# Attention, mish FFN and top-1 experts on one core: narrower expert slots, all weight splits on VectorE, logits in another buffer, the last slot's tiles one by one

## The chip, the cores and the metric

The kernel runs on one core of one Trainium2 chip. The metric is device time in microseconds of one execution, the median of several. Engines are named as in the profile: PE (TensorE, with its weight loads as PEld), DVE (VectorE), ACT (ScalarE), POOL (GpSimd) and SP (SyncE, which issues most DMAs).

## The reference

```python
def reference(q, k, v, w_in, w_out, w_gate, w_output_gate, w1, w2):
    # attention: 4 batches, 8 heads, 576 tokens, head size 64
    # heads 0-3: causal, window 32; heads 4-7: causal, every 4th key, window 128
    x = softmax(mask(q @ k.T / 8)) @ v            # -> x: 2304 x 512
    h = x @ w_in                                  # 512 -> 2048
    x = (h * tanh(log1p(exp(h)))) @ w_out         # 2048 -> 512
    logits = x @ w_gate                           # 8 experts
    e = argmax(logits); p = softmax(logits)[e]
    s = sigmoid(x @ w_output_gate)[e]
    return p * s * (relu(x @ w1[e]) @ w2[e])      # 512 -> 1024 -> 512
```

All data is float32.

## The kernel before, in words

**Precision.** Every float32 operand of a large matmul is split in two float32r parts, hi (a copy that ACT rounds) and lo (the difference), and a product takes three matmuls, hi·hi, hi·lo and lo·hi (PASS). `split` (L331) does it for a piece: ACT L332 writes hi, and L334 subtracts on DVE, or on POOL where `pool_lo` is set.

**First part (up to about 578 us).** The 2304 tokens go through in eight half-batches of 288. A step g is one block of 128 hidden columns of one half-batch: `l1` (L388, 12 matmuls of 288 columns into one of two PSUM tiles `hps`), the mish chain (ACT L395 exp, DVE L396, DVE L400, ACT L406 and L407, DVE L412, which frees `hps`, then `split` into ghi and glo), and, LAG = 3 steps later, `l2` (L431, 12 matmuls). The attention of the next half-batch is cut in small operations, and a hand-written loop (`take`) puts some of them between the halves of `l1` and `l2`. PE, DVE and ACT each run their instructions in the order in which the program was scheduled, so a late operation holds all behind it on its engine.

**Routing.** After a half-batch's last step its logits are made in pieces: `logits1` (8 matmuls of the transposed form, ACT L484 evicts them into the tile `lgT`), `logits2` (three transposes back, L491), `route1` and `route2` (the choice and each token's row number), `route3` (L555 transposes of 96 tokens, DVE L561 or ACT L559 copies them into a tile `row`, DVE L562 and L563 append the scale and the token's number) and `route4` (L582: POOL scatters the 96 rows into the DRAM array `buf`, which has a region of 2304 rows for each expert). The tiles `row`, `lgT`, `fill`, some gathered rows `xs` and the output rows `eo` all share one ring of three buffers (pool `rp`, tag "row"). `setup_rows` (L126) fills the first MOST rows of each region with zeros and an invalid token number.

**Experts (from about 578 us).** A slot is one expert, taken in order of its number of tokens; the expert of rank 2 comes first (slot 0: 256 rows at once, 128 late ones in `e_l1_late` with hi and lo side by side). CAPS gives each slot's number of rows; tokens above a cap go through the loop in `rest` (L808), which runs zero times on this input. Expert weights come in 64 loads of 512 KB (`e_load`, SP L664 and L667, a ring of four buffers shared with other loads), each split in two halves of 128x512 (`e_split`). Of the 128 halves 36 are subtracted on POOL: pieces 1, 3, 5 and 7 of slot 0 and pieces 3 and 7 of the other slots. The first eight pieces are split in the last steps of the first part. `e_l1` (L730) is 12 matmuls for each of 8 blocks f, with CAPS[q] moving columns; ACT L734 and DVE L735 evict. In slots 1, 3, 4 and 5 (COLUMNS) `e_l2` holds weights and moves CAPS[q] columns (L764, 12 matmuls a block, then transposes L803); in the others it holds the tokens and moves 512 weight columns (L772). `e_row` scales a tile of rows (ACT L780) and POOL scatters it to the output (L781).

Of the kernel before, what the change touches and what calls it, by code (L numbers as in the profile page):

```python
# [9 lines left out]
F32 = mybir.dt.float32  # L10
# [18 lines left out]
def tile_attn_mish_moe(ctx, tc, qkv, w_in, w_out, w_gate, w_og, w1, w2, out):  # L29
# [12 lines left out]
    NCH = HS // CH  # L42
    NP = HS // DIL
    ROW = DM + 2
    FCAP = 384
    CAPS = [FCAP, 440, 384, 336, 312, 288, 256, 256]
    PRE = 256
    COLUMNS = (1, 3, 4, 5)
    EGB = 2
# [278 lines left out]
                                       op0=ALU.logical_shift_right, op1=ALU.bitwise_or)  # L328
        return f.bitcast(F32)

    def split(hi, lo, src, pool_lo=False):  # L331
        nc.scalar.activation(out=hi, in_=src, func=AF.Copy)  # L332
        eng = nc.gpsimd if pool_lo else nc.vector
        eng.tensor_tensor(out=lo, in0=src, in1=hi.bitcast(F32), op=ALU.subtract)  # L334

    def w_split(n):
        kind, f = pieces[n]
# [136 lines left out]
    def logits1(j):  # L474

        R = rt[j]
        hl = R.pop("hl")
        ps = ps_a.tile([4 * E, HS], F32, tag="a", name="lgT")
        for kk in range(KD):
            for x in range(2):  # L480
                nc.tensor.matmul(out=ps, lhsT=wgs[:, kk, :], rhs=hl[x][:, kk, :],
                                 start=(kk == 0 and x == 0), stop=(kk == KD - 1 and x == 1))
        R["lgT"] = rp.tile([128, ROW], F32, tag="row", name="lgT")[0:4 * E, 0:HS]
        nc.scalar.activation(out=R["lgT"], in_=ps, func=AF.Copy)  # L484

    def logits2(j):
# [180 lines left out]
            nc.sync.dma_start(out=t.rearrange("p (k f) -> p k f", k=2), in_=src.rearrange("o (k p) f -> p (o k) f", p=128))  # L667
        es[q, i] = t

    def e_split(q, i, pool_lo=False):  # L670
        kind, hf = divmod(i, 4)
        if hf == 0:
            for a in range(2):
                ew[q, kind, a] = wp.tile([128, 4096], F32R, tag="w", name="we")
        c = slice(1024 * hf, 1024 * hf + 1024)
        t, hi, lo = es.pop((q, i)), ew[q, kind, 0][:, c], ew[q, kind, 1][:, c]
        if pool_lo:
            for h in (slice(0, 512), slice(512, 1024)):
                split(hi[:, h], lo[:, h], t[:, h], True)
        else:  # L680
            for c in (0, 512):
                split(hi[:, c:c + 512], lo[:, c:c + 512], t[:, c:c + 512], False)

    es_seq = [(q, i) for q in range(E) for i in range(NPC)]
    nload = [0]
# [7 lines left out]
    def e_splits_to(n, last=E * 8):  # L693
        while nsplit[0] < min(n, last, len(es_seq)):
            i = nsplit[0]
            e_loads_to(min(i + 3, last))
            e_split(*es_seq[i], pool_lo=i % 8 in ((1, 3, 5, 7) if i < 8 else (3, 7)))
            nsplit[0] += 1
            e_loads_to(min(i + 4, last))

# [36 lines left out]

    def e_l1_late(f, x):

        ps = ps_h.tile([128, 2, 128], F32, tag="h", name="eh")  # L740
        for kk in range(KD):
            c = kk * F2 + 128 * f
            for a in range(2):
                nc.tensor.matmul(out=ps, lhsT=ew[0, 0, a][:, c:c + 128], rhs=x[:, kk],
                                 start=(kk == 0 and a == 0), stop=(kk == KD - 1 and a == 1))
        t = mg.tile([128, 128], F32, tag="lt", name="lt", bufs=2)
        nc.vector.tensor_copy(t, ps[:, 0])
        nc.vector.tensor_tensor(out=t, in0=ps[:, 1], in1=t, op=ALU.add)
        g = mg.tile([128, 2, 128], F32R, tag=("egh", "egl")[f % 2], name="eg")
        gh, gl = g[:, 0], g[:, 1]  # L750
        nc.scalar.activation(out=gh, in_=t, func=AF.Relu)
        nc.vector.scalar_tensor_tensor(out=gl, in0=t, scalar=0.0, in1=gh.bitcast(F32), op0=ALU.max, op1=ALU.subtract)
        gt["e", 0, f] = (gh, gl)

    def e_l2(q, f, part):

# [16 lines left out]
                                 rhs=ew[q, 1, a][:, DM * f:DM * f + DM],  # L773
                                 start=(f == 0 and n == 0), stop=(f == NF2 - 1 and n == 2))

    def e_row(q, i, m, src):

        x = meta[q, 0][0:m, i // 128, :]
        o = rp.tile([128, DM], F32, tag="row", name="eo")
        nc.scalar.activation(out=o[0:m], in_=src, func=AF.Copy, scale=x[:, 0:1])  # L780
        ins = nc.gpsimd.indirect_dma_start(  # L781
            out=out[:, :], out_offset=bass.IndirectOffsetOnAxis(ap=x.bitcast(I32)[:, 1:2], axis=0),
            in_=o[0:m], in_offset=None, bounds_check=NT - 1, oob_is_err=False)
        apart("out", ins)
# [20 lines left out]
        return [lambda i=i, m=m: turn(i, m) for i, m in part]  # L805


    def rest():  # L808

        cnt = chosen["cnt"]  # L810
        caps = sm.tile([128, E], F32, name="caps")
# [27 lines left out]
        nc.vector.tensor_copy(rv, ri)  # L839
        mo_ctx.close()  # L840
        ot = ctx.enter_context(tc.tile_pool(name="ot", bufs=1, reuse_waits="tile"))
        n = nc.values_load(tn[0:1, 0:1], min_val=0, max_val=NT // 128 + E)
        w1r = w1.rearrange("e d f -> (e d) f")
        w2r = w2.rearrange("e f d -> (e f) d")
        with tc.For_i(0, n, 1):
# [60 lines left out]
    if True:  # L906
# [37 lines left out]
        for g in range(total + LAG):  # L944
            if g in begin:
                j, due = begin[g]
                pend += attention(j)
                rate[0] = len(pend) / (4 * NF)
                credit[0] = 0
            if g < total:  # L950
                j, f = steps[g][:2]
            nq = -(-len(pend) // max(1, due - g)) if g < total else 0

            def take(at):
                if 2 * NF <= g < total - NF:
                    credit[0] += rate[0]
                    n = int(credit[0] + 1e-6)
                    credit[0] -= n
                else:
                    n = (nq + 4 - at) // 4  # L960
                for _ in range(n):
                    if pend:
                        pend.pop(0)()
                for op in at_slot.pop((g, at), []):
                    op()
            w_to(max((i + 1 for i, x in enumerate(need) if x <= g), default=0), 80)
            if g < total:
                l1(g, 0)
                take(4)
                l1(g, 1)  # L970
            if 0 < g <= total:
                mish_c(g - 1)
            if g < total:
                mish_a(g)
            take(1)
            if 0 < g <= total:
                mish_d(g - 1)
            if g >= LAG:
                l2(g - LAG, 0)
                take(3)  # L980
                l2(g - LAG, 1)
                jj, ff, _, lst, _ = steps[g - LAG]
                if lst:
                    route0(jj)
                    if ff == NF - 1 and jj < NH - 1:
                        logits0(jj)
                        rq = routing(jj)
                        if jj == NH - 2:
                            rq += [choose_first, first_load, lambda: first_tr(0), lambda: first_tr(1)]
                        when, slot = (ROUTE, 4) if jj < NH - 2 else (ROUTE_SOON, 2)  # L990
                        for i, op in enumerate(rq):
                            at_slot.setdefault((g + 1 + when[i], slot), []).append(op)
            if g < total:
                mish_b(g)
            take(2)
            if g == FILLS - 6:
                nc.sync.dma_start(out=wg[:, :, 0:E], in_=w_gate.rearrange("(k p) e -> p k e", p=128))
                nc.sync.dma_start(out=wg[:, :, E:2 * E], in_=w_og.rearrange("(k p) e -> p k e", p=128))
            if g == FILLS:
                split(wgs[:, :, 0:2 * E], wgs[:, :, 2 * E:], wg, False)  # L1000
            if FILLS <= g < FILLS + E:
                setup_rows(g - FILLS)
            if j == NH - 1 and f >= 6 and g < total:
                e_splits_to(f - 7, 8)
# [8 lines left out]
        for f in range(NF2 + 1):  # L1013
            if f < NF2:
                e_l1(0, f, PRE, first[0], first[1], gp, (("ghi", 2), ("glo", 2)))
            if f >= 1:
                e_l2(0, f - 1, pre)
            if f == 4:
                (li, lm), = late
                x_load(0, li, lm, rp, "row")  # L1020
                xl = stp.tile([128, KD, 2, 128], F32R, tag="st", name="xl")
            if f == 7:
                x_tr(0, li, lm, xl[:, :, 0, :], xl[:, :, 1, :])
            e_splits_to(8 + f - 4)
# [6 lines left out]
    if True:  # L1031
# [23 lines left out]
        for q in range(1, E):  # L1055
# [5 lines left out]
            for f in range(NF2 + 1):  # L1061
                if f < NF2:
                    e_l1(q, f, CAPS[q], exh[q], exl[q], mg, (("egh", EGB), ("egl", EGB)))
                    e_splits_to(8 * (q + 1) + f + 1)
                if f >= 1:
                    e_l2(q, f - 1, tiles(q))
                if outs and f >= 1:
                    outs.pop(0)()
                if ops and f >= 3:
                    ops.pop(0)()  # L1070
            while ops:
                ops.pop(0)()
            outs = e_out(q, tiles(q))
    rest()


_INS = ['qkv', 'moe_w_in', 'moe_w_out', 'moe2_w_gate', 'moe2_w_output_gate', 'moe2_w1', 'moe2_w2']
# [59 lines left out]
```

## Time and profile before

| | |
|---|---|
| median of 3 runs | 842.54 us (842.39 to 846.82) |
| the profiled execution | 846.02 us |
| its span | 844.3 us |
| PE busy | 805.8 us, 95% of the span |
| DVE busy | 558.3 us, 66% |
| ACT busy | 501.8 us, 59% |
| POOL busy | 105.5 us, 12% |

The profile is of one execution, the second row of this table; 1.72 us of its time lie outside the span, and the median is 3.48 us under it. Shares of busy time are means over very different stages, so the prediction reads windows of the span and what each engine waited for there.

### The profile page before, as it was taken

The numbers are of one execution on the slowest core, as the hardware profiler recorded it, in microseconds if no ns is written. First come the engines' busy times: TensorE is split into PE (matmuls) and PEld (weight loads), VectorE is DVE, ScalarE is ACT, GpSimd is POOL, SyncE is SP. The second block draws the span as 40 slices with busy tenths as digits, with TensorE's granted clock in tenths as the row PEclk, the third lists the DMA queues.
The fourth block names the chain that finished last, engine by engine and source line by source line (L and its number), as shares of the span: only waits on it lengthen the run. The fifth ranks groups of instructions, "written<-read, shape, count | busy, mean of one in ns | idle before, by whom it ended". The sixth has DMA issues, their size and how long they took to land.

```text
span 844.3 us, 16623 instructions
## 1 busy us (share of the span) xinstructions
PE 805.8 (95%) x6205; PEld 751.9 (89%) x6205; DVE 558.3 (66%) x1473; ACT 501.8 (59%) x1419; POOL 105.5 (12%) x109
## 2 busy tenths in 40 slices
PE   7899999798999999999999999989999999999994
PEld 5779998798999999999999999989889989999993
DVE  5979999777767757767767767784772535543610
ACT  3677877675667667667666666661662644644611
POOL 4000000001100100100100000231240313313400
PEclk8989999899999999999999999999999999999997
DMA  9722459411110110111111000521882626536300
GB/s 344 271 80 75 151 159 312 121 37 60 53 55 31 53 56 30 51 39 49 44 35 58 23 10 2 181 73 48 285 286 68 212 82 234 171 113 228 123 24 18
DMA packets 39837, 91.69 MB, mean 109 GB/s; under 512 B 4643, under 2 KB 12835, under 8 KB 39756
## 3 DMA queue, kind: packets, MB, share of 16 engines
q1 hardware_dynamic: 36508, 81.16, 29.6%
q0 software_dynamic: 3248, 9.46, 3.3%
q8 instruction: 49, 0.80, 0.4%
q14 instruction: 32, 0.26, 0.1%
HBM read 73.91 MB, written 17.41 MB: 108 GB/s over the span
## 4 chain that ended last, share of the span: by engine, by line
PE 68%; DVE 12%; DMA 6%; issue 5%; ACT 5%; POOL 1%; SPq 1%; POOLq 0%; ACTq 0%; DVEq 0%
PE hps L388 20%; PE acc L431 19%; PE eh L730 8%; PE ecol L764 6%; DMA wst<-in_moe_w_in_dram 3%; PE o L264 3%; DMA est<-in_moe_w_dram 3%; PE eacc L772 2%; PE sc L218 2%; ACT pr L229 2%; PE tp L246 2%; DVE we L334 2%; ACT we L332 1%; DVE pr L226 1%; DVE nm L227 1%
## 5 line engine op out<-in xcount | busy, mean ns | idle before, releaser
L388 PE MATMUL hps<-xhi,w 128*128 128x288 f32 x1024 | 239.7, 306 | 6.4 <-DVE e L412 6.2
L388 PEld LDWEIGHTS hps<-xhi,w 128*128 128x128 f32 x1024 | 175.2, 191 | 11.7 <-DVE e L412 7.0
L431 PE MATMUL acc<-ghi,w 128*128 128x288 f32 x1024 | 172.5, 302 | 2.3 <-DVE x2T L449 1.3
L388 PE MATMUL hps<-xlo,w 128*128 128x288 f32 x512 | 153.0, 299 | 0.4 <-DVE xlo L271 0.3
L431 PEld LDWEIGHTS acc<-ghi,w 128*128 128x128 f32 x1024 | 145.9, 190 | 8.1 <-DVE x2T L449 2.3
L730 PE MATMUL eh<-exh,we 128*128 128x256 f32 (+5 forms) x448 | 108.6, 316 | 0.0
L388 PEld LDWEIGHTS hps<-xlo,w 128*128 128x128 f32 x512 | 98.2, 192 | 2.2 <-DVE xlo L271 1.8
L431 PE MATMUL acc<-glo,w 128*128 128x288 f32 x512 | 92.8, 297 | 3.1 <-DVE glo L334 3.1
L332 ACT ACTIVATE we<-est 128x512 fp32r<-128x512 f32 x128 | 74.4, 624 | 33.3 <-PE eh L730 16.4
L406 ACT ACTIVATE e<-e,two 128x288 f32<-128x288 f32 x128 | 68.1, 532 | 36.9 <-DVE e L400 36.0
L395 ACT ACTIVATE e<-hps 128x288 f32<-128x288 f32 x128 | 51.6, 404 | 55.0 <-PE hps L388 55.0
L334 DVE TENSOR_TENSOR we<-est,we 128x512 fp32r<-128x512 f32 x92 | 66.1, 755 | 25.2 <-ACT we L332 25.2
L431 PEld LDWEIGHTS acc<-glo,w 128*128 128x128 f32 x512 | 76.6, 190 | 3.7 <-DVE glo L334 3.4
L730 PEld LDWEIGHTS eh<-exh,we 128*128 128x128 f32 x448 | 77.2, 188 | 1.3
L332 ACT ACTIVATE ghi<-e 128x288 fp32r<-128x288 f32 x128 | 56.0, 438 | 31.9 <-PE acc L431 21.7
L582 POOL DMA_INDIRECT buf<-row,si x24 | 22.5, 936 | 417.5 <-DVE si L547 245.4
L735 DVE SCALAR_TENSOR_TENSOR eg<-eh,eg 128x256 fp32r<-128x256 f32 (+5 forms) x64 | 31.0, 484 | 64.2 <-ACT eg L734 64.1
L334 DVE TENSOR_TENSOR glo<-e,ghi 128x288 fp32r<-128x288 f32 x128 | 59.1, 462 | 20.1 <-PE acc L431 10.5
L412 DVE SCALAR_TENSOR_TENSOR e<-e,hps 128x288 f32<-128x288 f32 x128 | 57.4, 448 | 22.1 <-ACT e L407 21.8
L229 ACT ACTIVATE pr<-pr,nm 96x128 f32<-96x128 f32 (+2 forms) x168 | 62.0, 370 | 13.3 <-DVE nm L227 12.9
L730 PE MATMUL eh<-exl,we 128*128 128x256 f32 (+5 forms) x224 | 69.7, 311 | 0.0
L764 PE MATMUL ecol<-eg,we 128*128 128x440 f32 (+3 forms) x384 | 65.4, 320 | 0.5 <-DVE eg L735 0.5
(196 smaller groups left out, 1313.9 us busy)
## 6 DMA issues: line engine op xcount, KB each, us to landing
est<-in_moe_w_dram SPq DMA_DIRECT2D x64, 512.0 KB, 4.2
wst<-in_moe_w_in_dram SPq DMA_DIRECT2D x16, 512.0 KB, 9.6
wst<-in_moe_w_out_dram SPq DMA_DIRECT2D x16, 512.0 KB, 4.4
qkv<-in_qkv_dram SPq DMA_DIRECT2D x12, 608.0 KB, 3.6
qkv<-in_qkv_dram SPq DMA_DIRECT2D x14, 496.0 KB, 3.3
buf<-fill SPq DMA_DIRECT2D x8, 771.0 KB, 8.1
xs<-buf SPq DMA_DIRECT2D x19, 257.0 KB, 4.0
scq<-in_qkv_dram SPq DMA_DIRECT2D x4, 608.0 KB, 10.2
```

Source lines behind the costliest of these rows:

```text
L229: nc.scalar.activation(out=pr[:, h, u, :], in_=src[:, u, :], func=AF.Exp, bias=nm[0:m, h, u:u + 1], accum_out=su[0:m, h, u:u + 1])
L264: nc.tensor.matmul(out=o[64 * h:64 * h + 64, u, :], lhsT=vv, rhs=st["t", h][:, u, :], start=True, stop=True, skip_group_check=True)
L332: nc.scalar.activation(out=hi, in_=src, func=AF.Copy)
L334: eng.tensor_tensor(out=lo, in0=src, in1=hi.bitcast(F32), op=ALU.subtract)
L388: nc.tensor.matmul(out=hps[g], lhsT=w[:, a, kk, 128 * fl:128 * fl + 128], rhs=(xhi, xlo)[x][j][:, kk, :], start=(kk == 0 and n == 0), stop ...
L395: nc.scalar.activation(out=e, in_=hps[g], func=AF.Exp)
L406: nc.scalar.activation(out=r, in_=r, func=AF.Ln, scale=0.2, bias=two5)
L412: nc.vector.scalar_tensor_tensor(out=u, in0=u, scalar=2.5, in1=hps.pop(g), op0=ALU.subtract, op1=ALU.mult)
L431: nc.tensor.matmul(out=accs[j][m], lhsT=w[:, a, fl, 128 * m:128 * m + 128], rhs=gg[x], start=(first and n == 0), stop=(last and n == 2))
L730: nc.tensor.matmul(out=ps, lhsT=ew[q, 0, a][:, c:c + 128], rhs=(hi, lo)[x][:, kk, 0:n], start=(k == 0), stop=(k == 3 * KD - 1))
L735: nc.vector.scalar_tensor_tensor(out=gl, in0=ps, scalar=0.0, in1=gh.bitcast(F32), op0=ALU.max, op1=ALU.subtract)
L764: nc.tensor.matmul(out=accs["e", q][k], lhsT=ew[q, 1, a][:, c:c + 128], rhs=gg[x], start=(f == 0 and n == 0), stop=(f == NF2 - 1 and n == 2))
```

## The change

- `CAPS` goes from [384, 440, 384, 336, 312, 288, 256, 256] to [384, 424, 368, 336, 304, 280, 256, 232], and MOST, its largest, from 440 to 424.
- `split` loses `pool_lo`: all 128 halves of the expert weights are subtracted on DVE.
- `lgT` moves from the ring "row" of three buffers to the ring "pt" of two, which the attention's transposed probabilities use.
- In the last slot (q = 7) the `e_l2` matmuls of blocks 6 and 7 are done for one tile of rows after the other (`e_l2_end`), each tile's rows written right after; the second tile's eviction is shared by DVE and ACT.
- `rest` is cut in two: the count of tokens above the caps is made after slot 6, the loop stays at the end. `e_l1_late` takes its width from FCAP - PRE, which is 128 as before.

```diff
-    CAPS = [FCAP, 440, 384, 336, 312, 288, 256, 256]
+    CAPS = [FCAP, 424, 368, 336, 304, 280, 256, 232]
...
-    def split(hi, lo, src, pool_lo=False):
+    def split(hi, lo, src):
         nc.scalar.activation(out=hi, in_=src, func=AF.Copy)
-        eng = nc.gpsimd if pool_lo else nc.vector
-        eng.tensor_tensor(out=lo, in0=src, in1=hi.bitcast(F32), op=ALU.subtract)
+        nc.vector.tensor_tensor(out=lo, in0=src, in1=hi.bitcast(F32), op=ALU.subtract)
...
-        R["lgT"] = rp.tile([128, ROW], F32, tag="row", name="lgT")[0:4 * E, 0:HS]
+        R["lgT"] = ap.tile([4 * E, HS], F32, tag="pt", name="lgT")
         nc.scalar.activation(out=R["lgT"], in_=ps, func=AF.Copy)
...
-            e_split(*es_seq[i], pool_lo=i % 8 in ((1, 3, 5, 7) if i < 8 else (3, 7)))
+            e_split(*es_seq[i])
...
+    def e_l2_end(q, part):
+
+        for t, (i, m) in enumerate(part):
+            for f in (NF2 - 2, NF2 - 1):
+                for n, (a, x) in enumerate(PASS):
+                    nc.tensor.matmul(out=accs["e", q][t], lhsT=gt["e", q, f][x][:, i:i + m],
+                                     rhs=ew[q, 1, a][:, DM * f:DM * f + DM], start=False, stop=(f == NF2 - 1 and n == 2))
+            e_row(q, i, m, accs["e", q][t], t)
...
-    def e_row(q, i, m, src):
+    def e_row(q, i, m, src, alt=0):
...
-        nc.scalar.activation(out=o[0:m], in_=src, func=AF.Copy, scale=x[:, 0:1])
+        if alt % 2:
+
+            nc.vector.tensor_scalar(out=o[0:m, 0:DM // 2], in0=src[:, 0:DM // 2], scalar1=x[:, 0:1], scalar2=None, op0=ALU.mult)
+            nc.scalar.activation(out=o[0:m, DM // 2:], in_=src[:, DM // 2:], func=AF.Copy, scale=x[:, 0:1])
+        else:
+            nc.scalar.activation(out=o[0:m], in_=src, func=AF.Copy, scale=x[:, 0:1])
...
-                if f >= 1:
+                if f >= 1 and (q < E - 1 or f < NF2 - 1):
                     e_l2(q, f - 1, tiles(q))
...
-            outs = e_out(q, tiles(q))
-    rest()
+            if q < E - 1:
+                outs = e_out(q, tiles(q))
+                if q == E - 2:
+                    left = rest_count()
+            else:
+                e_l2_end(q, tiles(q))
+    rest(*left)
```

The first place is DVE's queue in the last steps of the first part, where slot 0's weights `we` are split among the mish chain (`e`) and its splits (`glo`). Before:

```order
L412 SCALAR_TENSOR_TENSOR e<-e,hps 128x288
L396 TENSOR_SCALAR e<-e 128x288
L400 TENSOR_TENSOR e<-e 128x288
L334 TENSOR_TENSOR we<-est,we 128x512
L334 TENSOR_TENSOR glo<-e,ghi 128x288
L334 TENSOR_TENSOR we<-est,we 128x512
L412 SCALAR_TENSOR_TENSOR e<-e,hps 128x288
L396 TENSOR_SCALAR e<-e 128x288
```

And in the change:

```order
L412 SCALAR_TENSOR_TENSOR e<-e,hps 128x288
L334 TENSOR_TENSOR we<-est,we 128x512
L396 TENSOR_SCALAR e<-e 128x288
L334 TENSOR_TENSOR we<-est,we 128x512
L400 TENSOR_TENSOR e<-e 128x288
L334 TENSOR_TENSOR glo<-e,ghi 128x288
L334 TENSOR_TENSOR we<-est,we 128x512 x3
L412 SCALAR_TENSOR_TENSOR e<-e,hps 128x288
```

The halves that POOL did now stand in DVE's own queue: five instead of two between two L412 here, and one of them between L412 and the next step's L396.

The second place is the ACT queue where `lgT` of the second half-batch is evicted, with the semaphores that each instruction waits for (DMASW0 is the queue of a POOL scatter). Before:

```order
L406 ACTIVATE e<-e,two_109 128x288 [waits DVE_49]
L407 ACTIVATE e<-e 128x288 [waits Activation_49]
L484 ACTIVATE lgT<-lgT 32x288 [waits DMASW0_49,PE_49]
L395 ACTIVATE e<-hps 128x288 [waits PE_49]
L406 ACTIVATE e<-e,two_109 128x288 [waits DVE_49]
```

And in the change:

```order
L406 ACTIVATE e<-e,two_109 128x288 [waits DVE_49]
L407 ACTIVATE e<-e 128x288 [waits Activation_49]
L484 ACTIVATE lgT<-lgT 32x288 [waits PE_49]
L395 ACTIVATE e<-hps 128x288 [waits PE_49]
L406 ACTIVATE e<-e,two_109 128x288 [waits DVE_49]
```

ACT no longer waits for the scatter. DVE's queue at the same place, in the change (before, the copy of the ids waited for DMASW1, the scatter after that one):

```order
L561 COPY row<-rows 96x512 [waits PE_49]
L412 SCALAR_TENSOR_TENSOR e<-e,hps 128x288 [waits Activation_49]
L563 COPY row<-ids 96x1 [waits DMASW0_49]
L396 TENSOR_SCALAR e<-e 128x288 [waits Activation_49]
L400 TENSOR_TENSOR e<-e 128x288 [waits DVE_49]
```

So the copy of the ids still waits for a scatter, the one that ACT waited for before.

## Rows read from the trace of the kernel before

**Rows 1.** Part 1 of the page: busy time of each engine over the span.
```profile
PE 805.8 (95%) x6205; PEld 751.9 (89%) x6205; DVE 558.3 (66%) x1473; ACT 501.8 (59%) x1419; POOL 105.5 (12%) x109
```

**Rows 2.** Windows: length, PE, PEld, DVE, ACT, POOL busy (count), granted clock, DMA share, GB/s.
```profile
145.00:160.00 15.00, 10.61 (x73) 9.59 (x72) 10.35 (x25) 8.29 (x20) 0.00 (x0) 0.77 0.71 214
204.50:215.36 10.86, 8.93 (x64) 8.10 (x63) 5.66 (x22) 5.38 (x24) 0.91 (x1) 0.84 0.26 100
211.00:213.00 2.00, 2.00 (x10) 1.66 (x10) 1.93 (x6) 1.01 (x5) 0.00 (x0) 0.50 0.00 0
273.43:280.32 6.89, 6.89 (x63) 6.45 (x62) 5.39 (x23) 5.71 (x26) 0.00 (x0) 1.00 0.01 2
547.00:563.00 16.00, 12.58 (x89) 11.65 (x88) 15.46 (x23) 11.43 (x26) 8.24 (x7) 1.00 0.34 98
595.00:605.00 10.00, 8.76 (x51) 7.11 (x51) 7.06 (x13) 7.15 (x15) 5.10 (x4) 1.00 0.67 215
605.00:832.00 227.00, 226.32 (x1427) 212.80 (x1427) 105.77 (x211) 105.25 (x213) 54.51 (x45) 1.00 0.46 154
```

**Rows 3.** Chain of waits: start, length, engine, output, line, count; slots 1 and 5.
```profile
623.32 2.40 PE ecol L764 x12
...
762.57 1.60 PE eh L730 x12
```

**Rows 4.** Timeline of PE in slot 7: start, length, instruction; 12 matmuls from the first to the second.
```profile
819.86 0.28 PE L730 MATMUL eh<-exh,we 128*128 128x256 f32 x1
...
821.28 1.54 PE L772 MATMUL eacc<-we,eg 128*128 128x512 f32 x6
```

**Rows 5.** Timeline of PE, last steps of the first part: in brackets idle before, and releaser.
```profile
549.31 0.40 PE L388 MATMUL hps<-xhi,w 128*128 128x288 f32 x1 [0.63 <-DVE e L412]
...
553.92 0.40 PE L388 MATMUL hps<-xhi,w 128*128 128x288 f32 x1 [1.18 <-DVE e L412]
...
558.86 0.40 PE L388 MATMUL hps<-xhi,w 128*128 128x288 f32 x1 [1.48 <-DVE e L412]
```

**Rows 6.** DVE by line and form, 545 to 562 us: busy, mean ns, idle before.
```profile
L400 DVE TENSOR_TENSOR e<-e 128x288 f32<-128x288 f32 x4 | 5.8, 1444 | 0.1
...
L396 DVE TENSOR_SCALAR e<-e 128x288 f32<-128x288 f32 x4 | 3.2, 810 | 0.7 <-ACT e L395 0.6
```

**Rows 7.** The same view, 563 to 575 us, where POOL splits nothing.
```profile
L400 DVE TENSOR_TENSOR e<-e 128x288 f32<-128x288 f32 x3 | 1.4, 459 | 0.1
L396 DVE TENSOR_SCALAR e<-e 128x288 f32<-128x288 f32 x2 | 0.6, 310 | 0.9 <-ACT e L395 0.9
```

**Rows 8.** One half's price: DVE timeline in slot 1, then POOL by line and form.
```profile
625.75 3.69 DVE L334 TENSOR_TENSOR we<-est,we 128x512 fp32r<-128x512 f32 x6
...
L334 POOL TENSOR_TENSOR we<-est,we 128x512 fp32r<-128x512 f32 x36 | 49.2, 1387 | 133.8 <-ACT we L332 133.7
```

**Rows 9.** Waits of SP's DMA queue from 570 us: total, times, longest.
```profile
SPq L667 <- POOL we L334: 17.4, 7, 4.7
```

**Rows 10.** Timeline where `lgT` of the second half-batch is evicted.
```profile
208.06 0.40 ACT L484 ACTIVATE lgT<-lgT 32x288 f32<-32x288 f32 x1 [4.18 <-DMA buf<-row,si]
...
208.52 0.93 PE L218 MATMUL sc<-qkv 64*72 64x104 f32 x14 [1.93 <-ACT lgT L484]
208.66 0.15 DVE L563 COPY row<-ids 96x1 int32<-96x1 int32 x1 [3.96 <-DMA buf<-row,si]
...
219.83 0.46 DVE L412 SCALAR_TENSOR_TENSOR e<-e,hps 128x288 f32<-128x288 f32 x1
```

**Rows 11.** Timeline of the end.
```profile
829.71 2.97 PE L772 MATMUL eacc<-we,eg 128*128 128x512 f32 x12
...
832.02 1.39 ACT L780 ACTIVATE eo<-eacc,meta 128x512 f32<-128x512 f32 x2 [1.72 <-PE eacc L772]
...
834.26 0.98 POOL L781 DMA_INDIRECT out_dram<-eo,meta  x1 [0.31 <-issue]
```

**Rows 12.** PE by line and form: attention scores, plain float32, 48 matmuls in the program.
```profile
L218 PE MATMUL sc<-qkv 64*72 64x104 f32 x96 | 6.0, 257 | 1.9 <-ACT lgT L484 1.9
```

More of the change, by code (lines that the diff above doesn't have):

```diff
@@ L668, in e_load, with e_split @@
         es[q, i] = t
-    def e_split(q, i, pool_lo=False):
+    def e_split(q, i):
         kind, hf = divmod(i, 4)
@@ L676, in e_split @@
         t, hi, lo = es.pop((q, i)), ew[q, kind, 0][:, c], ew[q, kind, 1][:, c]
[L677 to L682, printed above, removed]
+        for c in (0, 512):
+            split(hi[:, c:c + 512], lo[:, c:c + 512], t[:, c:c + 512])
     es_seq = [(q, i) for q in range(E) for i in range(NPC)]
@@ L738, in e_l1_late @@
     def e_l1_late(f, x):
-        ps = ps_h.tile([128, 2, 128], F32, tag="h", name="eh")
+        m = FCAP - PRE
+        ps = ps_h.tile([128, 2, m], F32, tag="h", name="eh")
         for kk in range(KD):
@@ L745, in e_l1_late @@
                                  start=(kk == 0 and a == 0), stop=(kk == KD - 1 and a == 1))
-        t = mg.tile([128, 128], F32, tag="lt", name="lt", bufs=2)
+        t = mg.tile([128, m], F32, tag="lt", name="lt", bufs=2)
         nc.vector.tensor_copy(t, ps[:, 0])
         nc.vector.tensor_tensor(out=t, in0=ps[:, 1], in1=t, op=ALU.add)
-        g = mg.tile([128, 2, 128], F32R, tag=("egh", "egl")[f % 2], name="eg")
+        g = mg.tile([128, 2, m], F32R, tag=("egh", "egl")[f % 2], name="eg")
         gh, gl = g[:, 0], g[:, 1]
@@ L805, in e_out, with rest_count @@
         return [lambda i=i, m=m: turn(i, m) for i, m in part]
-    def rest():
+    def rest_count():
         cnt = chosen["cnt"]
@@ L829, in rest @@
         nc.vector.tensor_copy(tn, tf)
+        return cnt, rem, nc.values_load(tn[0:1, 0:1], min_val=0, max_val=NT // 128 + E)
+    def rest(cnt, rem, n):
         li = sm.tile([128, 13], I32, name="li")
@@ L841, in rest @@
         ot = ctx.enter_context(tc.tile_pool(name="ot", bufs=1, reuse_waits="tile"))
-        n = nc.values_load(tn[0:1, 0:1], min_val=0, max_val=NT // 128 + E)
         w1r = w1.rearrange("e d f -> (e d) f")
@@ L999, in tile_attn_mish_moe @@
             if g == FILLS:
-                split(wgs[:, :, 0:2 * E], wgs[:, :, 2 * E:], wg, False)
+                split(wgs[:, :, 0:2 * E], wgs[:, :, 2 * E:], wg)
             if FILLS <= g < FILLS + E:
@@ L1020, in tile_attn_mish_moe @@
                 x_load(0, li, lm, rp, "row")
-                xl = stp.tile([128, KD, 2, 128], F32R, tag="st", name="xl")
+                xl = stp.tile([128, KD, 2, FCAP - PRE], F32R, tag="st", name="xl")
             if f == 7:
```

## The prediction

> **What bounds the kernel now.** I read the busy shares first: PE is busy 95% of the span and no other engine over 66% [rows 1]. So time is either PE's own work or one of its few waits, and the next view was the windows, to find where PE has holes [rows 2]. In the expert stage, 605 to 832 us, it is busy 226.32 of 227: what counts there is the number of columns that PE moves. Holes lie in three places that the change touches: 145 to 160 (transfers, granted clock 0.77), 204.5 to 215.36 (routing of the second half-batch) and 547 to 563 (the last steps of the first part). For the holes I read the timeline of PE and of the engine that it waited for [rows 5, 10], for prices the chain [rows 3] and groups by form [rows 6 to 8]. The sum is made against the profiled execution, 846.02 us; the median is 3.48 less.
>
> **Narrower slots.** Twelve matmuls of 440 columns take 2.40 us, twelve of 288 take 1.60 [rows 3]: 0.200 and 0.133 each, so 0.44 ns a column and no fixed part to speak of. Slot 1 loses 16 columns in 192 matmuls (both layers move tokens), slot 2 loses 16 in the 96 of its first layer, slots 4 and 5 lose 8 in 192 each: 7680 columns, 3.36 us. The second layers of slots 2 and 7 move 512 weight columns and gain nothing. Slot 7 loses 24 columns in 96 matmuls, from 256 to 232. At 256 columns twelve took 821.28 - 819.86 = 1.42 us, 0.118 each [rows 4]; by the slope the 96 save 1.0. No row shows a large float32r matmul under 256 columns, so this gain is bounded by 0 (the pace stays) and 1.0; I take 0.8, since the slope held over the whole range that rows show. Together **4.2 us**, and PE leaves nearly no idle time that could swallow it [rows 2]. The tokens all still fit, so the loop at the end stays empty; moving its count is free, as the engines do it beside PE's matmuls.
>
> The Trainium skill, page "TensorE: Matmul & The Clock Gate", section "Back-to-back issue gap", has the spacing of matmuls set by the weight load and the matmul together; it would put slot 7's gain anywhere under 1.0, which the bounds above hold already, and no run here shows the size.
>
> **Splits off POOL, last steps of the first part.** Between 547 and 563 DVE is busy 15.46 of 16 us [rows 2], and PE waited for DVE's L412, which frees its PSUM tile, 0.63, 1.18 and 1.48 us: 3.29 in all [rows 5]. DVE is full there because its own operations are slow while POOL splits: L400 takes 1.444 us on average against 0.459 a little later, L396 0.810 against 0.310 [rows 6, 7]. Four of each make 3.94 and 2.00: 5.9 us of DVE lost to eight halves on POOL of 1.387 each [rows 8]. The change puts these eight on DVE at 0.615 us (six in 3.69 [rows 8]): 4.9 us added for 5.9 removed. So DVE's work falls by about one microsecond, and I expect a step of it to be about 3.3 us where PE needs 3.2 plus what else it is given. The order shows five halves between two L412 in the first of these steps, 3.1 us of work, so a part of the wait may stay there. Between 0 and 3.3 I take **2.9 us**, nearest to the rows' balance of work.
>
> The Trainium skill, page "SBUF — State Buffer", section "Who interferes with whom", says that a DVE instruction with two SBUF inputs contends with a GpSimd instruction that reads SBUF, and that the loser of the shared port pair waits for all of it. The trace agrees in kind (L400 three times as long); as full blocking the eight halves would cost DVE 8 x 1.387 = 11.1 us, more than the 5.9 that these rows show, and the term would rise only to its end of 3.3, since PE waited no more than that.
>
> **Splits off POOL, later.** From 595 to 605 PE is busy 8.76 of 10 [rows 2] and waits for slot 0's last weights, some split on POOL at more than twice DVE's price: I take **0.4**, ends -0.5 (DVE's queue is late instead) and 1.2 (the whole hole). From 605 on DVE takes the other halves, 28 of the 36: at 0.615 about 17 us on top of 105.77 busy in 227, which fits on average. SP's queue waited 17.4 us for POOL before it could issue weight loads [rows 9]; that goes, but PE's missing time is 0.7 in all, so earlier weights are worth nothing. **0**, ends +0.7 and -3 (below).
>
> **The logits' buffer.** ACT's L484 waited 4.18 us for a scatter that still held a buffer of the ring, DVE's L563 3.96 for the next one; PE stood 1.93 [rows 10], and just after, the granted clock was 0.50, the 1.2 GHz level, from 211 to 213 [rows 2]. From 204.50 to 215.36 it did 64 matmul records in 10.86 us; the same stretch of a later half-batch took 6.89 for 63 [rows 2]: 3.97 us lost, the upper end. The change frees ACT, but DVE's queue still has the copy of the ids behind a scatter, now the first of the two, which landed at 208.06 where the second landed at 208.66 [rows 10]. So DVE is let go some 0.6 us earlier, and the mish chain behind it (L396, L412, then `hps`) with it; ACT is 4 us earlier with the attention's work. The lower end is 0.6. Whether PE still pauses long enough to lose the clock isn't in the rows; I take **1.0**, near the lower end, because the late DVE remains. The `pt` ring has only two buffers: a tile of logits held there stops an attention copy for some steps at worst, one copy of half a microsecond; the half-batches come with slack, so 0.
>
> **Fills.** MOST falls by 16 rows for 8 experts, 16 x 2056 B x 8 = 0.26 MB, in a window at 0.71 of the DMA engines and 214 GB/s [rows 2]: 1.2 us of transfers there, of which the weights on the path are a share; **0.3**, ends 0 and 1.2.
>
> **The end.** Before, the last twelve eacc matmuls start at 829.71; the first tile is complete after the ninth, the second after the twelfth, and ACT begins at 832.02 [rows 11]. Then two evictions of 0.69 and two POOL issues of 0.98 follow one another: POOL, not ACT, sets the end, and starts the second at 834.26, 1.28 after the first. In the change the first tile is complete after the seventh, about 0.5 us sooner. The halved second eviction is hidden behind POOL's first issue. **0.5**, ends 0.2 and 0.6.
>
> **Sum.** 4.2 + 2.9 + 0.4 + 0 + 1.0 + 0.3 + 0.5 = 9.3 us: 836.7 profiled, 833.2 as the median. The forecast's own range, 829.0 to 836.5, takes the upper ends of the logits' and the fills' terms, and at its slow end loses the wait of the last steps or most of the logits' and slot 7's gain.
>
> **Rivals.**
> *Slower: the last slot's matmuls drop out of the fast float32r pace under 256 columns.* Plain float32 products show what this would be: the scores of 64x104 stand with two records for each matmul (96 for 48 [rows 12]), and fourteen records took 0.93 us, 0.64 ns a column each [rows 10]. A matmul of 232 columns would be 2 x 232 x 0.64 ns = 0.30 us instead of 0.118, 96 times: 17 us lost instead of 0.8 gained, a time of **851**. It decides as soon as 232 columns cost over 0.21 us. For it: every large float32r matmul of this kernel moves at least 256. Against it: nothing in the slope from 288 to 440 hints at a step. The Trainium skill, page "FP8 and Floating Point Precision", section "TensorE Precision Notes", gives true FP32 four passes through the array; four passes at 0.44 ns a column would be 0.41 us a matmul and a time of about 862 (an estimate), and the two records here do not show four. Chance 0.14.
>
> *DVE becomes the bound in the slots.* Bursts of six halves stand in its queue between two evictions of `eg`: 3.69 + 0.4 = 4.1 us, where a block of a slot of 288 columns lasts 2 x 1.60 = 3.2 [rows 3, 8]. After some slack I price it at 0.5 us in each of six slots, 3 us, and with it goes the wait in the last steps (2.9) in part: **836.5 to 840.5**. For it: DVE already stands at 15.46 of 16 in one window. Against: a block's own two halves are 1.2 us, and before, the same burst at 625.75 cost PE nothing. Chance 0.24.
>
> *The change does less than it says*: the logits' wait only moves from ACT to DVE, and gains nothing. That is within the forecast's range (834.2).
>
> **How the numbers follow.** Forecast 0.58, DVE bound 0.24, slow last slot 0.14, better than 829 (the whole logits' and clock loss, fills and a shorter first part together) 0.04. The predicted time is 833.2; the range 829.0 to 840.5 holds the first two, 0.82. Half a per cent, 4.2 us, is about what a measurement of this kernel can tell from no change: under 838.3 is faster. The forecast and most of the DVE case make 0.77, the rest of the DVE case 0.09 the same, the slow slot 0.14.
>
> **What would show it.** Right: 232-column blocks at about 1.3 us for twelve; no PE wait on L412 over 0.5 us between 547 and 563, and L400 near 0.46; L484 without a DMA wait, L563 with one of about 3 us; ACT's first `eo` half a microsecond sooner against the last matmuls. Wrong: a last slot whose first-layer blocks take over 1.5 us, PE waits on DVE's L735 (`eg`) in slots 1 to 6, or a PE that starts the expert stage as late as before.

## The result and the profile after

The changed kernel takes 835.21 us, median of 9 runs (829.82 to 840.54), beside 843.78 for the kernel before (9 runs); the ratio of the two is 0.989, 95% interval 0.9858 to 0.9923. That is 9.3 us off, with an interval of 6.5 to 12.0. Executions of one kernel lie some 10 us apart, together with the granted clock averaged over each (0.987 to 0.977 in these nine), so medians of a dozen runs can't resolve one microsecond, and most of what follows is read from stretches of the traces.

Part 1 of the page of the changed kernel, beside [rows 1]:

```profile
PE 797.9 (96%) x6205; PEld 745.2 (90%) x6205; DVE 562.1 (68%) x1510; ACT 499.9 (60%) x1419; POOL 56.0 (7%) x73
```

DVE does 36 halves more, 22 us at the price of [rows 8], and is busy only 3.8 us longer. POOL's halves had hardly relieved it, since they slowed its other operations.

Windows of the changed kernel (columns as in [rows 2]; the last two are set earlier than there, since the work comes earlier):

```profile
145.00:160.00 15.00, 11.01 (x88) 10.07 (x87) 11.74 (x28) 9.33 (x27) 0.00 (x0) 0.89 0.62 201
204.50:213.50 9.00, 8.33 (x67) 7.63 (x63) 7.88 (x33) 5.89 (x25) 0.00 (x0) 1.00 0.06 22
543.00:558.00 15.00, 13.94 (x103) 13.47 (x102) 13.33 (x30) 12.36 (x30) 0.00 (x0) 1.00 0.32 103
605.00:818.00 213.00, 213.00 (x1369) 201.50 (x1369) 104.53 (x214) 98.24 (x199) 18.89 (x19) 1.00 0.45 152
```

PE now has no hole at all from 605 to 818. In the last steps of the first part, DVE is busy 13.33 of 15 us, where it was 15.46 of 16, although it does all the splits. Its operations there (by line and form, 540 to 558 us, against [rows 6, 7]):

```profile
L334 DVE TENSOR_TENSOR we<-est,we 128x512 fp32r<-128x512 f32 x14 | 9.2, 682 | 0.0
L400 DVE TENSOR_TENSOR e<-e 128x288 f32<-128x288 f32 x6 | 2.7, 452 | 0.1
L396 DVE TENSOR_SCALAR e<-e 128x288 f32<-128x288 f32 x6 | 1.8, 304 | 0.2 <-ACT e L395 0.2
```

L400 is back at 0.452 us from 1.444, L396 at 0.304 from 0.810. Of PE's three waits on L412 [rows 5] one is left (timeline of PE), in the step with five halves between two L412:

```profile
544.59 0.40 PE L388 MATMUL hps<-xhi,w 128*128 128x288 f32 x1 [0.98 <-DVE e L412]
```

At the logits of the second half-batch (timeline, against [rows 10]):

```profile
202.25 0.40 ACT L484 ACTIVATE lgT<-lgT 32x288 f32<-32x288 f32 x1 [0.82 <-PE lgT L481]
...
204.96 0.15 DVE L563 COPY row<-ids 96x1 int32<-96x1 int32 x1 [2.71 <-DMA buf<-row,si]
...
211.34 0.17 PE L539 MATMUL pos<-ohb,tri 96*96 96x24 bf16 x1 [0.67 <-DVE pt L250]
```

ACT waits for PE alone, DVE still 2.71 us for the first scatter, and PE once for 0.67. The clock stays at 1.00 there, the 2.4 GHz level.

In the last slot twelve matmuls of 232 columns go from 803.95 to 805.29, 1.34 us, 0.112 each (timeline of PE, against [rows 4]):

```profile
803.95 0.27 PE L726 MATMUL eh<-exh,we 128*128 128x232 f32 x1
...
805.29 1.09 PE L778 MATMUL eacc<-we,eg 128*128 128x512 f32 x4
```

And the end (timeline, against [rows 11]):

```profile
816.20 2.98 PE L757 MATMUL eacc<-we,eg 128*128 128x512 f32 x12
...
818.05 0.69 ACT L791 ACTIVATE eo<-eacc,meta 128x512 f32<-128x512 f32 x1 [1.29 <-PE eacc L757]
...
819.21 0.48 DVE L788 TENSOR_SCALAR eo<-eacc,meta 104x256 f32<-104x256 f32 x1 [2.02 <-PE eacc L757]
819.73 0.47 ACT L789 ACTIVATE eo<-eacc,meta 104x256 f32<-104x256 f32 x1 [0.99 <-DVE eo L788]
820.50 1.03 POOL L792 DMA_INDIRECT out_dram<-eo,meta  x1 [0.52 <-ACTq L859]
```

The first eviction starts 1.85 us after the start of the last twelve matmuls, where it was 2.31. The two halves of the second eviction run one after the other: ACT stands 0.99 us and is released by DVE's half, 0.04 us after that has ended, so the program orders the two writes into the one tile `eo`. POOL's second scatter starts 4.30 us after those matmuls' start, where it was 4.55.

### The profile page after: what moved, and what is told of

It reads as the page before. It is cut to its first block, busy times and chain, and to the rows that moved or that the text cites. A ratio compares the mean times of both kernels' runs of the same rounds, so it can differ in the third digit from the quotient of the medians.

```text
span 831.3 us, 16599 instructions
## 1 busy us (share of the span) xinstructions
PE 797.9 (96%) x6205; PEld 745.2 (90%) x6205; DVE 562.1 (68%) x1510; ACT 499.9 (60%) x1419; POOL 56.0 (7%) x73
## 4 chain that ended last, share of the span: by engine, by line
PE 69%; DVE 12%; DMA 7%; issue 5%; ACT 5%; SPq 1%; POOL 1%; POOLq 0%; DVEq 0%
PE hps L388 20%; PE acc L431 19%; PE eh L726 9%; PE ecol L770 7%; DMA est<-in_moe_w_dram 3%; PE eacc L778 3%; PE o L265 3%; DMA wst<-in_moe_w_in_dram 3%; PE sc L219 2%; ACT pr L230 2%; PE tp L247 2%; DVE nm L228 1%; DVE pr L227 1%; PE rows L555 1%; PE eh L741 1%
## 5 line engine op out<-in xcount | busy, mean ns | idle before, releaser
L726 PE MATMUL eh<-exh,we 128*128 128x424 f32 (+6 forms) x448 | 106.3, 312 | 0.0
L334 DVE TENSOR_TENSOR we<-est,we 128x512 fp32r<-128x512 f32 x128 | 83.0, 684 | 27.6 <-ACT we L333 27.3
L395 ACT ACTIVATE e<-hps 128x288 f32<-128x288 f32 x128 | 51.6, 404 | 54.3 <-PE hps L388 54.2
L412 DVE SCALAR_TENSOR_TENSOR e<-e,hps 128x288 f32<-128x288 f32 x128 | 57.4, 448 | 22.7 <-ACT e L407 22.4
L726 PE MATMUL eh<-exl,we 128*128 128x424 f32 (+6 forms) x224 | 68.9, 308 | 0.0
L770 PE MATMUL ecol<-eg,we 128*128 128x424 f32 (+3 forms) x384 | 63.9, 317 | 0.0
L731 DVE SCALAR_TENSOR_TENSOR eg<-eh,eg 128x256 fp32r<-128x256 f32 (+6 forms) x64 | 30.4, 474 | 49.4 <-ACT eg L730 49.2
L730 ACT ACTIVATE eg<-eh 128x256 fp32r<-128x256 f32 (+6 forms) x64 | 27.0, 421 | 60.5 <-PE eh L726 60.5
```

Source lines behind the costliest of these rows:

```text
L334: nc.vector.tensor_tensor(out=lo, in0=src, in1=hi.bitcast(F32), op=ALU.subtract)
L395: nc.scalar.activation(out=e, in_=hps[g], func=AF.Exp)
L412: nc.vector.scalar_tensor_tensor(out=u, in0=u, scalar=2.5, in1=hps.pop(g), op0=ALU.subtract, op1=ALU.mult)
L726: nc.tensor.matmul(out=ps, lhsT=ew[q, 0, a][:, c:c + 128], rhs=(hi, lo)[x][:, kk, 0:n], start=(k == 0), stop=(k == 3 * KD - 1))
L730: nc.scalar.activation(out=gh, in_=ps, func=AF.Relu)
L731: nc.vector.scalar_tensor_tensor(out=gl, in0=ps, scalar=0.0, in1=gh.bitcast(F32), op0=ALU.max, op1=ALU.subtract)
```

## The experiments

Stretches below are measured between the same instructions in each trace: the exp L395 of a step (counted from 0), the eviction of `eg` by ACT, POOL's last scatter. In us, the changed kernel twice (its second trace is the repeat described below):

| stretch | before | widths alone | splits alone | logits alone | end alone | changed | changed, again |
|---|---|---|---|---|---|---|---|
| step 26 to 30 (fills, last weights) | 23.65 | 22.31 | 22.22 | 23.91 | 21.81 | 22.13 | 23.17 |
| step 36 to 44 (second logits) | 39.27 | 37.65 | 37.38 | 36.91 | 37.44 | 36.51 | 36.77 |
| step 120 to 127 (last steps) | 27.20 | 27.21 | 24.98 | 27.45 | 27.35 | 24.65 | 24.47 |
| first `eg` of slot 0 to first of slot 1 | 43.38 | 42.97 | 42.58 | 43.44 | 43.52 | 43.35 | 42.35 |
| first `eg` of slot 1 to last of slot 7 | 208.89 | 205.91 | 208.00 | 208.74 | 209.16 | 203.36 | 203.13 |
| last `eg` to the last scatter's issue | 4.35 | 4.35 | 4.35 | 4.35 | 4.11 | 4.11 | 4.11 |

A kernel that leaves a stretch as it was shows how far that stretch moves by itself: the slots by 0.4 us (208.74 to 209.16), the last steps by 0.25, but the steps at the fills by 2.1 (21.81 to 23.91).

**Each part alone, added to the kernel before.**

*Widths:*

```diff
-    CAPS = [FCAP, 440, 384, 336, 312, 288, 256, 256]
+    CAPS = [FCAP, 424, 368, 336, 304, 280, 256, 232]
```

> The kernel before with the new widths alone (CAPS, and MOST with it). My theory: 4.2 us less from columns and 0.3 from fills, so about 4.5 us under the kernel before, and twelve matmuls of 232 columns in slot 7 take about 1.34 us, as in the changed kernel. Rival (the last slot under 256 columns is slow): slower than before. Rival (the gain of the change is not the columns but the splits and the logits): under 2 us.

Measured: ratio 0.9982 (0.9951 to 1.0014), medians 843.39 against 844.37. No gain beyond the interval: 1.5 us by the ratio, so by the medians the rival with under 2 us would stand, and only the stretches tell the parts from each other. The slots, where the columns lie, are 2.98 us shorter instead of 4.2. The slow-last-slot rival falls: its twelve matmuls take 819.44 - 818.10 = 1.34 us. What is missing stands in the timeline of PE of this kernel:

```profile
657.03 2.14 PE L772 MATMUL eacc<-we,eg 128*128 128x512 f32 x8 [0.45 <-DVE eg L735]
...
697.09 1.80 PE L764 MATMUL ecol<-eg,we 128*128 128x336 f32 x10 [0.44 <-DVE eg L735]
...
781.33 1.42 PE L772 MATMUL eacc<-we,eg 128*128 128x512 f32 x5 [0.67 <-DVE eg L735]
```

With POOL still splitting, DVE's evictions come late in slots 2, 3 and 6. Up to PE's last matmuls its idle time is these three waits, 1.56 us (window below), where before it was 0.7 [rows 2], most of it in slot 3 as here (second line, timeline of PE before):

```profile
605.00:824.50 219.50, 217.94 (x1396) 204.97 (x1395) 101.35 (x198) 101.31 (x206) 54.19 (x45) 1.00 0.44 150
...
703.39 1.81 PE L764 MATMUL ecol<-eg,we 128*128 128x336 f32 x10 [0.54 <-DVE eg L735]
```

So some 0.9 us of the missing gain are new waits, in slots 2 and 6.

*Splits:*

```diff
-            e_split(*es_seq[i], pool_lo=i % 8 in ((1, 3, 5, 7) if i < 8 else (3, 7)))
+            e_split(*es_seq[i])
```

> The kernel before with all splits on VectorE, nothing else. My theory: 3.3 us less (2.9 in the last steps of the first part, 0.4 in slot 0), L400 back near 0.46 us, nothing from 605 us on. Rival (DVE becomes the bound in the slots): the last steps gain 2 to 3 us but the slots lose it again, with PE waits on DVE's eg, in sum within 1 us of before.

Measured: ratio 0.994 (0.9906 to 0.9974), 839.31. The last steps are 2.2 us shorter, slot 0 up to slot 1 0.8, the other slots 0.9 (0.7 to 1.2 against the three traces with the old splits and widths): they don't lose it again, they gain, with the old widths too. Slot 0's 0.8 is within what that stretch moves by itself (42.35 and 43.35 in the two traces of the changed kernel). Two of the waits on L412 are left, 0.44 and 0.98 us.

*Logits:*

```diff
-        R["lgT"] = rp.tile([128, ROW], F32, tag="row", name="lgT")[0:4 * E, 0:HS]
+        R["lgT"] = ap.tile([4 * E, HS], F32, tag="pt", name="lgT")
```

> The kernel before with the logits' tile in the other ring, nothing else. My theory: 1.0 us less, DVE's copy of the ids still waits about 3 us for the first scatter. Rival (the wait only moves from ACT to DVE): no change, PE still stands near 2 us there. Rival (the half clock after the wait goes too): 2.7 us less, as the traces of the two kernels show at this place.

Measured: ratio 1.0005 (0.9978 to 1.0033), 844.33: nothing that a median of twelve runs shows. The stretch is 36.91 us. Against the profiled execution of before (39.27) that is 2.4 less, but in the three other kernels without this edit it is 37.65, 37.38 and 37.44: their PE waited 1.28, 1.27 and 1.25 us there instead of 1.93, and their clock did not fall. In the kernel with the widths alone (timeline of PE, then a window):

```profile
205.40 0.93 PE L218 MATMUL sc<-qkv 64*72 64x104 f32 x14 [1.28 <-ACT lgT L484]
...
200.00:215.00 15.00, 13.55 (x111) 12.31 (x110) 10.41 (x40) 7.76 (x31) 2.13 (x3) 1.00 0.26 82
```

So the lasting part is 0.5 to 0.7 us here and 0.6 to 1.1 in the changed kernel. The rest of the difference at this place between the two first traces, 1.6 to 1.9 us, is the longer wait and the fallen clock [rows 2] of one execution of the kernel before, which no other trace has here.

*The end:* `e_l2_end`, the shared eviction and `rest_count` of the diff above, with the old widths, splits and logits.

> The kernel before with the last slot's tiles done one by one, the shared eviction and the earlier count, nothing else (CAPS as before). My theory: 0.5 us less: the first eviction begins about 0.85 us sooner against the last matmuls' start, as 3 of 12 matmuls follow it no longer, but POOL's two issues of 0.98 and the landing stay. Rival (the landing of the second scatter sets the end and varies by more than that): within 0.3 us.

Measured: ratio 0.999 (0.9957 to 1.0022), 843.94. From the last `eg` to the last scatter 4.11 us instead of 4.35: 0.24, half of what was forecast, since the second tile's two half evictions stand one behind the other. Whether it reaches the median is below what these runs can tell.

By their ratios the four parts make 7.0 us together; the changed kernel, with all four, 9.3. The intervals alone would allow that, but the row of the slots says where it comes from: 2.98 and 0.89 apart, 5.53 and 5.76 together. Once the splits are off POOL, the widths give 4.6 (208.00 to 203.36).

**Parts taken back from the changed kernel.** POOL gets 28 halves of the later slots back:

```diff
-            e_split(*es_seq[i])
+            e_split(*es_seq[i], pool_lo=i >= 8 and i % 8 in (3, 7))
```

> The changed kernel with POOL doing the lo halves of pieces 3 and 7 of slots 1 to 7 again (28 halves), all else as changed. What the prediction held (these 28 are worth 0): no change to the changed kernel, ratio 0.989. Rival, from the kernel with the widths alone, whose PE waited 0.45, 0.44 and 0.67 us for eg in slots 2, 3 and 6 where the changed kernel waits nowhere over 0.1: in narrower slots POOL's halves come too late, and 1 to 2 us of the widths' gain are lost again, ratio 0.990 to 0.992, with such waits in the trace.

Measured: ratio 0.9932 (0.9904 to 0.996), 837.45, and slots 1 to 7 take 206.02 us instead of 203.36. The rival holds, and the size is above it: 2.7 us by the stretch, and the ratio is beyond the 0.992 that it set. The same waits stand at the same slots; the last of them, in slot 6, on the timelines of DVE, POOL and PE:

```profile
775.02 2.98 DVE L335 TENSOR_TENSOR we<-est,we 128x512 fp32r<-128x512 f32 x3
777.92 0.41 DVE L732 SCALAR_TENSOR_TENSOR eg<-eh,eg 128x256 fp32r<-128x256 f32 x1
778.26 1.43 DVE L335 TENSOR_TENSOR we<-est,we 128x512 fp32r<-128x512 f32 x1
```

```profile
776.05 3.09 POOL L335 TENSOR_TENSOR we<-est,we 128x512 fp32r<-128x512 f32 x2 [14.65 <-ACT we L333]
```

```profile
778.39 0.96 PE L779 MATMUL eacc<-we,eg 128*128 128x512 f32 x3 [0.67 <-DVE eg L732]
```

While POOL splits, from 776.05 to 779.14, DVE's three halves take 2.98 us (1.9 alone) and the next one 1.43; the eviction behind them is late, and PE waits. DVE is busy 555.6 us in this kernel and 562.1 in the changed one: 28 halves on POOL take only 6.5 us off DVE, 0.23 each, where one costs it 0.615. The halves that stay on DVE are the ones that become slower, 810 ns on average instead of 684 (DVE by line and form, 600 to 820 us, this kernel and then the changed one):

```profile
L335 DVE TENSOR_TENSOR we<-est,we 128x512 fp32r<-128x512 f32 x75 | 57.8, 810 | 21.4 <-ACT we L333 21.0 <-issue 0.2
L334 DVE TENSOR_TENSOR we<-est,we 128x512 fp32r<-128x512 f32 x100 | 64.8, 684 | 23.1 <-ACT we L333 22.7
```

The same for the eight halves of slot 0:

```diff
-            e_split(*es_seq[i])
+            e_split(*es_seq[i], pool_lo=i in (1, 3, 5, 7))
```

> The changed kernel with POOL doing the lo halves of pieces 1, 3, 5 and 7 of slot 0 again (8 halves), all else as changed. My theory: the three waits of PE on L412 at the end of the first part come back, 2 to 2.5 us in the stretch of the last steps, and nothing changes in the slots; ratio 0.991 to 0.993. Rival (what is gained in the last steps is given back in slot 0, whose weights land no sooner): the last steps lose 2 us, slot 0 gains 1 back, ratio 0.989 to 0.991.

Measured: ratio 0.9922 (0.9889 to 0.9954), 837.3. Step 120 to 127 takes 28.52 us instead of 24.65, 3.9 more where 2 to 2.5 were expected (and 1.3 more than in the kernel before), and the waits are back, four of them (timeline of PE, then DVE by line and form, 540 to 557 us):

```profile
541.23 0.40 PE L389 MATMUL hps<-xhi,w 128*128 128x288 f32 x1 [0.45 <-DVE e L413]
...
545.94 0.40 PE L389 MATMUL hps<-xhi,w 128*128 128x288 f32 x1 [1.26 <-DVE e L413]
...
550.53 0.40 PE L389 MATMUL hps<-xhi,w 128*128 128x288 f32 x1 [1.16 <-DVE e L413]
...
555.47 0.40 PE L389 MATMUL hps<-xhi,w 128*128 128x288 f32 x1 [1.48 <-DVE e L413]
...
L401 DVE TENSOR_TENSOR e<-e 128x288 f32<-128x288 f32 x4 | 5.8, 1444 | 0.1
...
L397 DVE TENSOR_SCALAR e<-e 128x288 f32<-128x288 f32 x4 | 3.2, 808 | 0.7 <-ACT e L396 0.6
```

L401, the L400 of before, takes 1.444 us again. DVE, with eight halves fewer to do, is busy 565.2 us in this kernel, 3.1 more than in the changed one: here POOL's help costs it time. Slot 0 up to slot 1 takes 42.95, between the two traces of the changed kernel (43.35 and 42.35), so no clear part of the gain is given back there. Slots 1 to 7 take 204.79 us, where no change was expected: in slot 6 PE waits 0.60 us for ACT and 0.29 for DVE, behind a weight that landed late.

```profile
785.79 0.63 ACT L333 ACTIVATE we<-est 128x512 fp32r<-128x512 f32 x1 [2.67 <-DMA est<-in_moe_w_dram]
```

POOL splits nothing there; why the weight was late is not shown. The kernels that leave the slots as in the changed one take 202.82 to 203.36.

**A last slot of 192 rows**, to see what its matmuls do further under 256 columns:

```diff
-    CAPS = [FCAP, 424, 368, 336, 304, 280, 256, 232]
+    CAPS = [FCAP, 424, 368, 336, 304, 280, 256, 192]
```

> The changed kernel with the last slot at 192 instead of 232 rows (its 177 tokens still fit). If the pace follows the columns (0.44 ns each), twelve first-layer matmuls of the last slot take 12 x 0.094 = 1.1 us; if a floor holds that the 232-column matmuls (0.112 us each, not 0.108 as the slope gives) already touch, they stay at 1.25 to 1.34. If matmuls far under 256 columns lose the fast pace, over 2 us.

Measured (one execution, 833.93): the timeline of PE gives 803.90 - 802.58 = 1.32 us for twelve.

```profile
802.58 0.25 PE L726 MATMUL eh<-exh,we 128*128 128x192 f32 x1
...
803.90 1.57 PE L778 MATMUL eacc<-we,eg 128*128 128x512 f32 x6
```

0.110 us each at 192 columns, 0.112 at 232, 0.118 at 256. From 232 to 192 columns twelve matmuls save 0.02 us, where 0.44 ns a column would save 0.21: there is a floor near 0.110, and below 232 columns a narrower slot of this form gains next to nothing. The Trainium skill, page "TensorE: Matmul & The Clock Gate", section "LDWEIGHTS (loading the stationary operand)", gives the nanoseconds of a weight load as its columns divided by 1.2; for 128 columns that makes 107 ns, an estimate from the page. The measured floor lies close to it, but the loads' own records are 188 ns long here and overlap, and no run changes the load alone, so that the load sets the floor is not shown.

**What the change left.** The ids are made to depend on the row numbers, so that their copy no longer stands ahead of time in DVE's queue:

```diff
+        idj = sm.tile([CH, NCH], I32, tag="idj", name="idj")
+        nc.vector.scalar_tensor_tensor(out=idj, in0=si, scalar=0, in1=ids[:, j * NCH:j * NCH + NCH], op0=ALU.mult, op1=ALU.add)
...
-        nc.vector.tensor_copy(row.bitcast(I32)[0:CH, DM + 1:DM + 2], ids[:, j * NCH + c:j * NCH + c + 1])
+        nc.vector.tensor_copy(row.bitcast(I32)[0:CH, DM + 1:DM + 2], R["idj"][:, c:c + 1])
```

> The changed kernel with the copy of the token ids made to depend on the row numbers (the ids of a half-batch are formed from si by one small DVE operation), so that it no longer stands early in DVE's queue waiting for a scatter. If DVE's wait of 2.71 us at 205 is what is left of the logits' stall: that wait is gone, the stretch from the second half-batch's logits on is 0.7 to 2 us shorter, ratio 0.987 to 0.988. If PE has other work there anyway: no change to the changed kernel (0.989).

Measured: ratio 0.9871 (0.9835 to 0.9907), 833.28. No copy of ids waits for a scatter at the second logits, and step 36 to 44 takes 35.50 us, 1.0 to 1.3 less than in the two traces of the changed kernel. By medians the two can't be told apart.

The fills moved behind the weight loads:

```diff
-            if FILLS <= g < FILLS + E:
-                setup_rows(g - FILLS)
+            if FILLS + 9 <= g < FILLS + 13:
+                setup_rows(2 * (g - FILLS - 9))
+                setup_rows(2 * (g - FILLS - 9) + 1)
```

> The changed kernel with the fills of the token regions issued after the last weight load of the first part (two regions a step from step 27 instead of one a step from step 18); the bytes are the same. If the fills hold back the weights that PE waits for at 150 us (2.73 and 1.26 us of waits, then 3.4 us at the 1.2 GHz level): these waits shrink and the time falls by 3 to 6 us, ratio 0.982 to 0.986. If the weights are late by their own volume: no change to the changed kernel. If the fills now land after the first scatter wants to go (199 us): that scatter is late and the gain is lost there.

Measured: ratio 0.9842 (0.9811 to 0.9873), 831.9. That is in the expected range, but the interval meets that of the changed kernel, and the same fills do not repeat it in the next kernel. The place is only half cured. In the changed kernel DVE waits for a weight's transfer, and PE twice behind it (timelines of DVE and PE):

```profile
147.90 0.43 DVE L324 TENSOR_SCALAR wf<-wst 128x512 int32<-128x512 int32 x1 [1.75 <-DMA wst<-in_moe_w_in_dram]
...
149.96 0.40 PE L431 MATMUL acc<-glo,w 128*128 128x288 f32 x1 [2.73 <-DVE glo L334]
151.62 0.56 PE L388 MATMUL hps<-xhi,w 128*128 128x288 f32 x1 [1.26 <-DVE e L412]
```

With the fills moved, neither DVE nor ACT shows a wait for a transfer from 135 to 160 us, and one wait of PE is left, which ends on another engine:

```profile
153.88 0.61 PE L388 MATMUL hps<-xhi,w 128*128 128x288 f32 x1 [3.02 <-ACT w L333]
```

So the weights land sooner, and what comes last now is a weight's split. The first scatter is not late. Step 26 to 36 takes 46.02 us instead of 47.19 and 48.24 in the two traces of the changed kernel. The second of these has the granted clock lower, 0.77 against 0.89 (windows of the changed kernel's second trace, then of this kernel):

```profile
145.00:160.00 15.00, 10.80 (x78) 9.74 (x77) 10.90 (x26) 8.37 (x22) 0.00 (x0) 0.77 0.56 184
145.00:160.00 15.00, 11.98 (x95) 11.23 (x94) 12.45 (x32) 9.83 (x30) 0.00 (x0) 0.89 0.42 139
```

The eleven traces that leave the fills where they were have 46.58 to 48.97 us in this stretch. The gain is 0.6 us against the fastest of them; how much more of it lasts is not shown.

Both together, and the changed kernel once more beside them:

> The changed kernel with both additions, ids that depend on the row numbers and fills after the last weight load. If the two places are independent: the stretch at the logits about 1 us shorter and the stretch from 150 to 190 us 1 to 2 us shorter than in the changed kernel, ratio 0.980 to 0.985. If one only moves the wait to the other: no better than the better of the two alone.

> The changed kernel once more, unaltered, beside the runs that are compared with it: ratio to the kernel before 0.986 to 0.992 as measured first; its stages should repeat within 0.3 us from 170 us on, apart from the slot 0 stretch, which hangs on transfers.

Measured: both 0.9865 (0.9819 to 0.991), 834.12; the changed kernel again 0.9881 (0.9839 to 0.9923), 834.39. The profiled execution of both has the shortest span of all (827.4 us); its stretches keep both gains (step 36 to 44 35.51, step 26 to 36 46.19, under the eleven traces above), so neither wait only moved to the other place. But medians of six runs do not show it to be faster than the changed kernel, and it isn't claimed. Of the stretches of the changed kernel, the last steps, the slots and the end repeat within 0.3 us, the one at the logits too; slot 0 and the steps at the fills differ by 1.0 each.

## Why the prediction was right

The forecast was 9.3 us under the kernel before and the measurement is 9.3 by the ratio; 835.21 lies in the range, 2.0 above the 833.2 forecast: the kernel before took 843.78 us beside it and not 842.54, and the two medians lie 8.6 apart. The places were right, but that the sum agrees to the tenth is luck: a term put at nothing made up for others that were too large.

- **Narrower slots, 4.2.** The columns are worth nearly what the slope says: with the widths alone slots 4 and 5, where little else changes, shrink by 0.63 and 0.60 us against 0.67 each, and slot 7's eight blocks by 0.08 each, 0.64 against the 0.8 taken. But alone they gave 2.98 in the slots. The step that failed is "PE leaves nearly no idle time that could swallow it": narrower slots shorten the time in which DVE must evict, and with POOL splitting DVE was late in slots 2 and 6.
- **Last steps, 2.9.** 2.2 alone, 2.6 to 2.7 in the changed kernel, and taking it back costs more than all of it again. The balance (5.9 us lost to POOL's company, 4.9 added) held. The remaining wait of 0.98 is the step with five halves, as the working said; the sign "no PE wait on L412 over 0.5 us" was missed by it.
- **Slot 0, 0.4.** Between 0.0 and 1.0 in two traces of the same kernel; not resolved.
- **Later splits, 0.** This term was mis-sized. It is 0.9 us with the old widths and 2.7 with the new ones (the kernel with the 28 halves back on POOL). I looked for what POOL's halves cost SP's queue and for PE's missing 0.7 us, and did not use here the rows that carried the term before it: the same slowing of DVE.
- **Logits, 1.0.** 0.5 to 1.1, with DVE's wait left as forecast (2.71 against some 3). The stretch at the 1.2 GHz level in [rows 2] belongs to that execution.
- **Fills, 0.3.** Not shown: the kernels with the splits alone and the end alone, with the old fills, have 22.22 and 21.81 us in that stretch, and the changed kernel's two traces differ by 1.0.
- **The end, 0.5.** 0.24: "hidden behind POOL's first issue" was wrong, as the half on ACT waited for the half on DVE, and POOL 0.52 us for both.

The rivals: the slow last slot is refuted by 0.112 us a matmul. DVE as the bound is refuted by a window without a hole in PE; its price was the wrong way round, since DVE was nearer its bound with POOL's help than without it. By the Trainium skill, page "SBUF — State Buffer", section "Who interferes with whom", two-input DVE instructions contend with a GpSimd instruction that reads SBUF; the trace agrees, with L400 at 1.444 us beside POOL and 0.452 without it, and a half on POOL relieves DVE of 0.23 us instead of 0.615.

## What to carry to other kernels

Before work is shared between VectorE and GpSimd, compare the mean duration of VectorE's own operations while GpSimd runs and while it does not: here a subtraction given to GpSimd in the slots saved VectorE 0.23 us of 0.615, and took 1.4 us itself; in the last steps of the first part it cost VectorE more than it saved. Two edits to one stage are not a sum when one shortens the time in which the other's wait must fit: the widths gained what their columns are worth only once the evictions came in time. And a stall with a fallen clock behind it, seen in one profiled execution, should be looked for in a second one before it enters a sum.

## What the runs showed of the hardware that was not expected

Float32r matmuls with 128 weight columns came no closer than 0.110 us on average when they moved 192 columns instead of 232 (0.112); 0.44 ns a column, counted down from 232, would give 0.094. VectorE's tensor_scalar with one input was slowed beside GpSimd as well, from 0.304 to 0.808 us on average in the same steps, not only the operations with two.
